# Ten of the 32 pieces of w_out decoded in MoE slots 2 to 5 and kept in DRAM, decode steps at fixed places, and the last selection ahead of its table

## The chip, the cores and the metric

The kernel runs on one core of a Trainium2 chip. The metric is the device time of one execution in microseconds, the median of several runs. A profiled execution has a time of its own, and its span runs from the first to the last instruction. The engines are TensorE (PE in the rows, PEld its weight loads), VectorE (DVE), ScalarE (ACT), GpSimd (POOL) and SyncE (SP), which issues most of the DMAs. Each engine works through its own instructions in order.

## The reference

Three layers in a row; the data are float32, but the last layer's weights come as float64.

```python
# 1: windowed attention, batch 4, 8 heads, 576 positions, 64 wide
attn = softmax(where(mask, q @ k.T / 8, -1e9))      # plain heads, then heads with dilation 4
x = (attn @ v).transpose(0, 2, 1, 3).reshape(2304, 512)
# 2: mixture of experts, one expert of 8 for each token
logits = x @ w_gate + modality_bias[modality_id]
e = argmax(logits); gate = softmax(logits)[e]
x = gate * (relu(x @ w1[e]) @ w2[e])                # w1: 512 x 1024, w2: 1024 x 512
# 3: the last layer
h = relu(x @ w_in)                                  # w_in: 512 x 2048
out = (h * h) @ w_out                               # w_out: 2048 x 512
```

## The kernel before, in words

All matrix products run on values split into a high and a low part (`hi`, `lo`), three matmuls for each product: hi x hi, hi x lo, lo x hi.

**Attention** is pipelined over 48 units of 96 queries (`schedule`, units counted by `i`, `nu` = 48). As the tokens of a batch are done, a side task routes them: `route` finds each token's expert and its place among that expert's tokens, and its end fills a table from slot and row to token (one-hot rows `rhot`, `val`, one matmul into `psi`, then `tbl`). `select` then finds which expert and which column of the table each MoE slot has (`esel`), and writes `itab`, from which `Moe.begin` on GpSimd reads a slot's token numbers (`sc`) and gathers its rows (`gx`). The side task yields a cost for every step, and `LATE[b]` zeros hold it back for as many units ahead of the table's matmul.

**The MoE** works on slots of 128 tokens of one expert, 18 or more in all (`Moe.main(j)`): layer one (`l1`, 24 matmuls, a yield after every third), transposing of the next slot's rows (`tx`, giving `xh` and `xl`), layer two of the slot before (`l2`, 24 matmuls), transposing of the hidden rows (`th`, giving `hth` and `htl`). Where a slot has another expert, its weights are loaded on SyncE (`stage`) and split on ScalarE and VectorE (`split`), both guarded by a branch. Slots 0 to 5 run between the last units of attention and after them (`moe.slots(0, NA)` as `fill`), slots 6 to 17 in a second loop in `body`; slots beyond these run under a branch (`extras`), and one does here.

**Decoding.** Float64 weights are turned into float32 pairs in pieces of 128 x 256 numbers. A step of the generator `decode` issues the DMA of one piece (`raw`) on SyncE and works on earlier pieces: an absolute value on ScalarE (`dm`), four passes on VectorE (`da`), the high part on ScalarE (`woh` or `wih`) and the low part, a subtraction, on GpSimd (`wol` or `wil`). The 32 pieces of w_in are decoded in slots 6 to 17, one step at each yield of cost 0 in the second loop. The 32 pieces of w_out, two to each 128-row block f of w_out, are decoded in block 0 of the last stage.

**The last stage** (`Ffn.run`) takes 6 blocks of 384 tokens. For each block and each of 16 values f: `l1` (12 matmuls of 384 columns, three banks in turn), `h1` (ReLU on ScalarE into `fr`, square into `fsq`), `h2` (`fhh` on ScalarE, `fhl` on VectorE), and with a lag of two to six values of f `l2` (9 matmuls of 512 columns, which need `woh` and `wol` of that f). In block 0 the order is written by hand, with two or three decode steps to each f. The squares of block 0 with f above 3 are on GpSimd, all others on VectorE. `Ffn.prep(1)` transposes block 1's rows near the end of block 0.

Of the kernel before, what the change touches and what calls it, by code (L numbers as in the profile page):

```python
# [26 lines left out]
FF = 2048  # L27
# [36 lines left out]
@with_exitstack  # L64
def body(ctx, tc, ins, out):
    nc = tc.nc
    const = ctx.enter_context(tc.tile_pool(name="const", bufs=1))
    dram = ctx.enter_context(tc.tile_pool(name="dram", bufs=1, space=bass.MemoryType.DRAM))
    psum = ctx.enter_context(tc.tile_pool(name="psum", bufs=1, space=PSUM))
    g = Ctx()  # L70
    g.tc, g.nc, g.ins, g.out = tc, nc, ins, out
    g.xd = dram.tile([NT, XW], F32, name="xd")
    g.ya = dram.tile([NA * 128, XW], F32, name="ya")
    g.yb = dram.tile([NT - NA * 128 + 128, XW], F32, name="yb")
    g.bk = [psum.tile([128, 512], F32, name=f"bk{i}") for i in range(8)]
    g.ident = const.tile([128, 128], F32, name="ident")
    g.iota = const.tile([128, NCOL], F32, name="iota")
    g.esel = const.tile([1, 4, NSLOT], I32, name="esel")
    g.nsl = const.tile([1, 1], I32, name="nsl")

    with ExitStack() as mctx:
        moe = Moe(g, mctx)
        with ExitStack() as actx:
            att = Attention(g, actx)
            att.warm(9)
            with tc.manual_schedule():
                schedule(att, moe)
# [12 lines left out]
        ffn.run()  # L100
# [11 lines left out]
def schedule(att, moe):  # L112
    nu = B * UPB
    moe.banks((2, 4), (4, 2), (2, 2), (7, 7))
    side, fc, sc, hold, nxt, due = None, 0.0, 0.0, 0, 0, 0
    i = 0
# [70 lines left out]
    run(side or ())  # L187
    if due:
        moe.ready = NSLOT
        moe.pump()  # L190


class Attention:
    def __init__(self, g, ctx):
# [235 lines left out]
    def route(self, b):  # L430
# [98 lines left out]
        if b:  # L529
            off = new([128, NCOL], "roff")  # L530
            nc.vector.tensor_scalar(out=off, in0=psi, scalar1=float(b * S), scalar2=float(b * S), op0=ALU.mult, op1=ALU.min)
            nc.vector.tensor_tensor(out=self.tbl, in0=self.tbl, in1=off, op=ALU.add)

    def select(self, j0, n):
# [97 lines left out]
        it = g.moe.itab[{0: 0, 2: 1, 6: 2}[j0]]  # L632
        yield 0.12
        nc.vector.tensor_scalar(out=it, in0=self.tbl, scalar1=-1.0, scalar2=0.0, op0=ALU.add, op1=ALU.max)
        for j in range(j0, j0 + n):
            g.moe.itab_of[j] = it


class Moe:
# [80 lines left out]
    def l1(self, j):  # L720
        nc = self.g.nc
        for hf in range(2):
# [3 lines left out]
            for c in range(4):  # L726
                for a, w in ((self.xh, self.wh[0]), (self.xh, self.wl[0]), (self.xl, self.wh[0])):
# [4 lines left out]
                    if k % 3 == 0:  # L732
                        yield 0.65
# [16 lines left out]
    def l2(self, j):  # L750
# [83 lines left out]
NB, TB = 6, 3  # L834
NF = FF // 128
DN = 256
LAG0, LAG = 6, 2


class Ffn:  # L840
    def __init__(self, g, ctx):
# [9 lines left out]
        jobs = [(wi[:, :, 2 * w * i:2 * w * i + 2 * w], self.wih[:, :, w * i:w * i + w], self.wil[:, :, w * i:w * i + w])  # L851
                for i in range(FF // w)]
        self.steps = itertools.chain(self.decode(jobs), self.prep0())

    def decode(self, jobs):
        nc, dp = self.g.nc, self.pool
        n = DN
        raws, vals = {}, {}
        for i in range(len(jobs) + 5):
            if i < len(jobs):  # L860
                src = jobs[i][0]
                raws[i] = dp.tile([128, n, 2], I32, tag="raw", name="raw", bufs=3)
                nc.sync.dma_start(out=raws[i].rearrange("p n two -> p (n two)").rearrange("p (c x) -> p c x", c=src.shape[1]), in_=src)
            new, old, done = i - 2, i - 3, i - 4
            if 0 <= new < len(jobs):
                m = dp.tile([128, n], F32, tag="m", name="dm", bufs=2)
                nc.scalar.activation(out=m, in_=raws[new][:, :, 1].bitcast(F32), func=AF.Abs)  # L867
                a = dp.tile([128, n], I32, tag="a", name="da", bufs=4)
                nc.vector.tensor_scalar(out=a, in0=raws[new][:, :, 1], scalar1=3, scalar2=0x3FFFFFF8,  # L869
                                        op0=ALU.logical_shift_left, op1=ALU.bitwise_and)  # L870
                vals[new] = (a, m)
            if old in vals:
                a = vals[old][0]
                nc.vector.scalar_tensor_tensor(out=a, in0=raws.pop(old)[:, :, 0], scalar=29, in1=a, op0=ALU.logical_shift_right, op1=ALU.bitwise_or)  # L874
            if new in vals:
                a = vals[new][0]
                nc.vector.scalar_tensor_tensor(out=a, in0=raws[new][:, :, 1], scalar=-0x40000000, in1=a, op0=ALU.bitwise_and, op1=ALU.bitwise_or)  # L877
            if old in vals:
                a, m = vals[old]
                nc.vector.scalar_tensor_tensor(out=a.bitcast(F32), in0=m, scalar=TINY, in1=a.bitcast(F32), op0=ALU.is_ge, op1=ALU.mult)  # L880
            if done in vals:
                _, hi, lo = jobs[done]
                v = vals.pop(done)[0].bitcast(F32).rearrange("p (c f) -> p c f", c=hi.shape[1])
                nc.scalar.activation(out=hi, in_=v, func=AF.Copy)  # L884
                nc.gpsimd.tensor_tensor(out=lo, in0=v, in1=hi.bitcast(F32), op=ALU.subtract)  # L885
            yield
# [62 lines left out]
    def h1(self, blk, f):  # L949
# [5 lines left out]
        (nc.gpsimd if blk == 0 and f > 3 else nc.vector).tensor_tensor(out=s, in0=r, in1=r, op=ALU.mult)  # L955
# [11 lines left out]
    def run(self):  # L967
# [3 lines left out]
        def pool(name, bufs):  # L971
# [6 lines left out]
        steps = self.decode([(wo[:, f:f + 1, 2 * h * DN:2 * (h + 1) * DN], woh[:, f:f + 1, h * DN:(h + 1) * DN], wol[:, f:f + 1, h * DN:(h + 1) * DN])  # L978
                             for f in range(NF) for h in range(DM // DN)])
# [104 lines left out]
```

## Time and profile before

| | us |
|---|---|
| median of 3 runs (813.43 to 816.45) | 816.21 |
| profiled execution, its time | 815.87 |
| profiled execution, its span | 814.1 |
| TensorE busy | 784.6 |
| VectorE busy | 418.9 |
| ScalarE busy | 325.1 |
| GpSimd busy | 173.9 |
| mean granted TensorE clock, share of full speed | 0.99 |

Busy times are sums over the whole span. The kernel goes through stages with different limits, so a stage is read from its own window. A matmul's end is modelled, so a stretch in which TensorE is shown busy may still contain short waits; the length of a stretch with known work tells more.

### The profile page before, as it was taken

What the parts mean: (1) busy time and instruction counts of PE and PEld (TensorE: products, weight loads), DVE (VectorE), ACT (ScalarE), POOL (GpSimd) and SP (SyncE); (2) the same over time, 40 slices, a digit from 0 to 9 for tenths busy, and PEclk for the clock granted to TensorE, in tenths of its full rate; (3) what the DMA queues carried; (4) which work ended last, traced back from release to release, by engine and by line L of the source; (5) the groups of instructions that cost most, each with busy time, mean ns of one, the idle gap of its engine ahead of it and who ended that gap; (6) DMA issues with size and microseconds to landing.
All of it is one profiled execution on the core that took longest, in us unless ns stands there. A gap on an engine that the chain in (4) does not pass through costs nothing.

```text
span 814.1 us, 12599 instructions
## 1 busy us (share of the span) xinstructions
PE 784.6 (96%) x4273; PEld 671.7 (83%) x4273; DVE 418.9 (51%) x1124; ACT 325.1 (40%) x779; POOL 173.9 (21%) x234
## 2 busy tenths in 40 slices
PE   8999987899999999998989899999999999999996
PEld 5888866788888888887877799989989989998995
DVE  5787888444257777441799942242242233224222
ACT  5777766232245554541444522232232222223221
POOL 4254731231123333110255610010000001001001
PEclk9999998999999999999999999999999999999999
DMA  7766681201234443722245410010001001001001
GB/s 225 188 177 163 177 279 43 68 27 46 72 118 119 140 130 100 247 91 72 80 115 147 127 39 26 1 52 27 1 13 39 27 14 39 1 0 39 1 1 39
DMA packets 44810, 67.40 MB, mean 83 GB/s; under 512 B 6816, under 2 KB 28672, under 8 KB 44224
## 3 DMA queue, kind: packets, MB, share of 16 engines
q1 hardware_dynamic: 38720, 50.75, 21.6%
q0 software_dynamic: 3280, 10.76, 4.3%
q10 hardware_dynamic: 2736, 4.99, 1.6%
q8 instruction: 35, 0.57, 0.3%
q14 instruction: 39, 0.32, 0.1%
HBM read 129.65 MB, written 14.44 MB: 177 GB/s over the span
## 4 chain that ended last, share of the span: by engine, by line
issue 40%; DVE 5%; PE 2%; DMA 2%; POOL 1%; ACT 1%; POOLq 0%; ACTq 0%; DVEq 0%; SPq 0%
DMA raw<-in_wo 2%; POOL out L995 1%; DVE da L880 1%; PE bk L945 1%; DVE fhl L964 1%; DVE da L874 1%; DVE da L869 1%; PE bk L758 1%; DVE da L877 1%; PE bk L990 1%; ACT dm L867 0%; ACT woh L884 0%; DVE fsq L955 0%; DVE yl L932 0%; DVE fout L994 0%
## 5 line engine op out<-in xcount | busy, mean ns | idle before, releaser
L955 DVE TENSOR_TENSOR fsq<-fr 128x384 f32<-128x384 f32 x84 | 46.9, 559 | 173.3 <-ACT fr L953 173.3
L945 PE MATMUL bk<-yh,wih 128*128 128x384 f32 x384 | 130.7, 340 | 3.2 <-ACTq L827 1.6
L945 PE MATMUL bk<-yl,wih 128*128 128x384 f32 x384 | 130.3, 339 | 1.3 <-DVE yl L932 1.3
L945 PE MATMUL bk<-yh,wil 128*128 128x384 f32 x384 | 129.9, 338 | 0.0
L953 ACT ACTIVATE fr<-bk 128x384 f32<-128x384 f32 x96 | 46.9, 488 | 187.9 <-PE bk L945 187.3
L990 PE MATMUL bk<-woh,fhh 128*128 128x512 f32 x288 | 114.6, 398 | 2.7 <-ACT woh L884 2.7
L990 PE MATMUL bk<-wol,fhh 128*128 128x512 f32 x288 | 113.4, 394 | 2.9 <-POOL wol L885 2.9
L990 PE MATMUL bk<-woh,fhl 128*128 128x512 f32 x288 | 113.3, 393 | 0.0
L995 POOL DMA_INDIRECT out<-fout,fidx x18 | 18.1, 1006 | 323.3 <-DVE fout L994 320.5
L945 PEld LDWEIGHTS bk<-yh,wih 128*128 128x128 f32 x384 | 72.6, 189 | 8.3 <-ACT yh L931 2.2
L964 DVE TENSOR_TENSOR fhl<-fsq,fhh 128x384 fp32r<-128x384 f32 x96 | 55.4, 578 | 45.0 <-ACT fhh L963 44.7
L945 PEld LDWEIGHTS bk<-yl,wih 128*128 128x128 f32 x384 | 72.7, 189 | 5.8 <-DVE yl L932 2.6
L945 PEld LDWEIGHTS bk<-yh,wil 128*128 128x128 f32 x384 | 72.7, 189 | 0.0
L963 ACT ACTIVATE fhh<-fsq 128x384 fp32r<-128x384 f32 x96 | 50.4, 525 | 50.2 <-DVE fsq L955 48.7
L990 PEld LDWEIGHTS bk<-wol,fhh 128*128 128x128 f32 x288 | 54.1, 188 | 14.2 <-POOL wol L885 5.9
L728 PE MATMUL bk<-w1h,xh 128*128 128x512 f32 x152 | 64.1, 421 | 0.8 <-DVE htl L744 0.8
L990 PEld LDWEIGHTS bk<-woh,fhl 128*128 128x128 f32 x288 | 54.0, 188 | 12.9 <-DVE fhl L964 0.4
L990 PEld LDWEIGHTS bk<-woh,fhh 128*128 128x128 f32 x288 | 54.1, 188 | 12.2 <-ACT woh L884 4.2
L728 PE MATMUL bk<-w1l,xh 128*128 128x512 f32 x152 | 61.6, 405 | 0.0
L728 PE MATMUL bk<-w1h,xl 128*128 128x512 f32 x152 | 61.5, 404 | 0.0
L758 PE MATMUL bk<-w2h,hth 128*128 128x512 f32 x152 | 61.0, 401 | 0.0
L758 PE MATMUL bk<-w2h,htl 128*128 128x512 f32 x152 | 59.5, 391 | 0.0
(173 smaller groups left out, 1375.9 us busy)
## 6 DMA issues: line engine op xcount, KB each, us to landing
st<-in_w SPq DMA_DIRECT2D x41, 2048.0 KB
raw<-in_wi SPq DMA_DIRECT2D x32, 256.0 KB
raw<-in_wo SPq DMA_DIRECT2D x32, 256.0 KB
v<-in_v SPq DMA_DIRECT2D x7, 780.0 KB
q<-in_q SPq DMA_DIRECT2D x7, 576.0 KB
kd<-in_k SPq DMA_DIRECT2D x14, 288.0 KB
xd<-x SPq DMA_DIRECT2D x40, 96.0 KB
yb<-y ACTq DMA_DIRECT2D x13, 256.5 KB
```

The source lines that it names most:

```text
L728: nc.tensor.matmul(ps, a[:, c, :], w[:, c, sl], start=k == 0, stop=k == 11)
L758: nc.tensor.matmul(ps, a[:, c, :], w[:, c, :], start=k == 0, stop=k == 23)
L869: nc.vector.tensor_scalar(out=a, in0=raws[new][:, :, 1], scalar1=3, scalar2=0x3FFFFFF8, op0=ALU.logical_shift_left, op1=ALU.bitwise_and)
L874: nc.vector.scalar_tensor_tensor(out=a, in0=raws.pop(old)[:, :, 0], scalar=29, in1=a, op0=ALU.logical_shift_right, op1=ALU.bitwise_or)
L877: nc.vector.scalar_tensor_tensor(out=a, in0=raws[new][:, :, 1], scalar=-0x40000000, in1=a, op0=ALU.bitwise_and, op1=ALU.bitwise_or)
L945: nc.tensor.matmul(ps, w[:, c, f * 128:(f + 1) * 128], a[:, c, :], start=k == 0, stop=k == 11)
L953: nc.scalar.activation(out=r, in_=ps, func=AF.Relu)
L955: (nc.gpsimd if blk == 0 and f > 3 else nc.vector).tensor_tensor(out=s, in0=r, in1=r, op=ALU.mult)
L963: nc.scalar.activation(out=hh, in_=s, func=AF.Copy)
L964: nc.vector.tensor_tensor(out=hl, in0=s, in1=hh.bitcast(F32), op=ALU.subtract)
L990: nc.tensor.matmul(acc[t], a[:, sl], w[:, f, :], start=f == 0 and j == 0, stop=f == NF - 1 and j == 2)
L995: dma = nc.gpsimd.indirect_dma_start(out=out, out_offset=bass.IndirectOffsetOnAxis(ap=self.idx[:, i:i + 1].bitcast(U32), axis=0), in_=o, i ...
```

## The change

The change has four parts. First, ten pieces of w_out (f = 0 to 4, `NE` = 5) are decoded by a new class `Early` while slots 2 to 5 run, stored to two DRAM tensors (`wod`), and loaded from there into `woh` and `wol` at the start of block 0 (`back`). Block 0 decodes the other 22, with one or two steps to each f. Second, a decode step is taken at marked yields (`MARK`): after the third matmul of each half of layer one and after the third and the fifteenth of layer two, four in a slot, for w_in too. Third, `route` is cut into `route`, `onehots` and `table`, and a new `batch` strings them together, so that only for the last batch `select` stands ahead of the table (`LATE` goes from 7 to 4 zeros there). Fourth, all squares are on VectorE. The pools of attention that only its units use are closed earlier, to make room for `Early`.

```diff
-LATE = (5, 5, 2, 7)
+LATE = (5, 5, 2, 4)
+    g.wod = [dram.tile([NE, 128, DM], F32, name=f"wo{i}") for i in range(2)]
...
             for cost in moe.slots(NA, NTT):
-                if not cost:
+                if cost == MARK:
                     ffn.side()
...
             else:
                 fc -= c
+                if early and c == MARK:
+                    early.step()
...
+        if i == nu + 6:
+            att.units.close()
+            early = Early(g)
...
-            side = itertools.chain(att.route(nxt), att.select(*WAVES[nxt - 1]) if nxt else ())
+            side = att.batch(nxt)
...
+    def batch(self, b):
+        moe = self.g.moe
+        yield from self.route(b)
+        if b < B - 1:
+            yield from self.table(b)
+        if b:
+            j0, n = WAVES[b - 1]
+            yield from self.select(j0, n)
+            for j in range(j0, j0 + n):
+                moe.itab_of[j] = moe.itab[b - 1]
+        if b == B - 1:
+            yield from self.table(b)
+        if b:
+            yield 0.12
+            self.g.nc.vector.tensor_scalar(out=moe.itab[b - 1], in0=self.tbl, scalar1=-1.0, scalar2=0.0, op0=ALU.add, op1=ALU.max)
...
                     if k % 3 == 0:
-                        yield 0.65
+                        yield MARK if k == 3 else 0.65
...
                 if k % 3 == 0 and k < 24:
-                    yield 0.65
+                    yield MARK if k in (3, 15) else 0.65
...
+class Early:
...
+        jobs = [(wo[:, f:f + 1, 2 * h * DN:2 * (h + 1) * DN], self.halves) for f in range(NE) for h in range(DM // DN)]
+        self.steps = decode(g.nc, self.pool, jobs, self.store)
...
+    def halves(self):
+        return [self.pool.tile([128, 1, DN], F32R, tag=t, name=t) for t in ("eh", "el")]
...
+    def store(self, i, hi, lo):
+        f, h = divmod(i, DM // DN)
+        for d, t in zip(self.g.wod, (hi, lo)):
+            self.g.nc.sync.dma_start(out=d[f, :, h * DN:(h + 1) * DN], in_=t[:, 0, :].bitcast(F32))
...
-        (nc.gpsimd if blk == 0 and f > 3 else nc.vector).tensor_tensor(out=s, in0=r, in1=r, op=ALU.mult)
+        nc.vector.tensor_tensor(out=s, in0=r, in1=r, op=ALU.mult)
...
+        def back(*fs):
+            for f in fs:
+                for t, d in zip((woh, wol), g.wod):
+                    nc.sync.dma_start(out=t[:, f, :].bitcast(F32), in_=d[f])
...
                     self.l1(0, i)
-                if i != 1:
+                if i < NE:
+                    back(i)
+                if i != 2:
                     next(steps, None)
                 if i:
                     self.h2(0, i - 1)
-                if i != 1:
-                    next(steps, None)
                 self.h1(0, i)
-                if i > 2 and i % 2:
+                if i > 2 and i % 4:
                     next(steps, None)
```

What stands in the engines' queues is shown at three places; numbers after a name tell tiles apart.

SyncE at the start of block 0: first the kernel before, where the loads of w_out for decoding begin at once.

```order
L863 DMA raw_6628<-in_wo 128x512 [waits DMAHW4_49,DVE_49,PE_49]
L863 DMA raw_6630<-in_wo 128x512 [waits DMAHW5_49]
L863 DMA raw_6656<-in_wo 128x512 [waits DMAHW6_49]
L863 DMA raw_6667<-in_wo 128x512 [waits DMAHW4_49,DMAHW7_49,DVE_49,Activation_49]
L863 DMA raw_6692<-in_wo 128x512 [waits DMAHW0_49,DMAHW5_49,DVE_49,Activation_49]
```

The same place in the changed kernel, with the ten loads from `wo0` and `wo1`.

```order
L1050 DMA woh_6784<-wo0_66 128x512 [waits DMAHW3_49,DMAHW4_49,DMAHW2_49,DMAHW5_49,DMAHW1_49,DMAHW6_49,DMAHW0_49,DMAHW7_49,DVE_49,Activation_49]
L1050 DMA wol_6785<-wo1_67 128x512 [waits DMAHW3_49,PE_49]
L881 DMA raw_6790<-in_wo 128x512
L1050 DMA woh_6784<-wo0_66 128x512
L1050 DMA wol_6785<-wo1_67 128x512 [waits DMAHW6_49]
L881 DMA raw_6798<-in_wo 128x512
L1050 DMA woh_6784<-wo0_66 128x512 [waits DMAHW0_49]
L1050 DMA wol_6785<-wo1_67 128x512 [waits DMAHW1_49]
L1050 DMA woh_6784<-wo0_66 128x512 [waits DMAHW2_49]
L1050 DMA wol_6785<-wo1_67 128x512 [waits DMAHW3_49]
L881 DMA raw_6844<-in_wo 128x512 [waits DMAHW4_49]
```

The first raw piece now stands behind a load that waits for TensorE, and the third is the eleventh in the queue.

VectorE in block 0, from `fhl` of f = 7 to `fhl` of f = 8, in the kernel before.

```order
L964 TENSOR_TENSOR fhl_6974<-fsq_6928,fhh_6973 128x384
L869 TENSOR_SCALAR da_6981<-raw_6930 128x256
L874 SCALAR_TENSOR_TENSOR da_6966<-raw_6915,da_6966 128x256
L877 SCALAR_TENSOR_TENSOR da_6981<-raw_6930,da_6981 128x256
L880 SCALAR_TENSOR_TENSOR da_6966<-dm_6964,da_6966 128x256
L869 TENSOR_SCALAR da_7034<-raw_6962 128x256
L874 SCALAR_TENSOR_TENSOR da_6981<-raw_6930,da_6981 128x256
L877 SCALAR_TENSOR_TENSOR da_7034<-raw_6962,da_7034 128x256
L880 SCALAR_TENSOR_TENSOR da_6981<-dm_6979,da_6981 128x256
L964 TENSOR_TENSOR fhl_7042<-fsq_6990,fhh_7041 128x384
```

The same place in the changed kernel.

```order
L1029 TENSOR_TENSOR fhl_7078<-fsq_7032,fhh_7077 128x384
L1020 TENSOR_TENSOR fsq_7083<-fr_7081 128x384
L887 TENSOR_SCALAR da_7127<-raw_7034 128x256
L892 SCALAR_TENSOR_TENSOR da_7070<-raw_7015,da_7070 128x256
L895 SCALAR_TENSOR_TENSOR da_7127<-raw_7034,da_7127 128x256
L898 SCALAR_TENSOR_TENSOR da_7070<-dm_7068,da_7070 128x256
L1029 TENSOR_TENSOR fhl_7135<-fsq_7083,fhh_7134 128x384
```

One decode step is gone from between them, and the square has come in. Elsewhere in the block there are two steps where three or two stood.

VectorE in slot 4, where the last batch's table is finished, in the kernel before.

```order
L528 TENSOR_TENSOR tbl_146<-bk5_71,tbl_146 128x144
L531 TENSOR_SCALAR roff_2938<-bk5_71 128x144
L532 TENSOR_TENSOR tbl_146<-tbl_146,roff_2938 128x144
L544 TENSOR_SCALAR sci_2941<-carry_141 1x8
L547 TENSOR_SCALAR scj_2943<-sci_2941 1x8
L550 TENSOR_TENSOR sav_2945<-scj_2943,taken_143 1x8
```

The same place in the changed kernel.

```order
L551 TENSOR_TENSOR tbl_151<-bk5_73,tbl_151 128x144
L554 TENSOR_SCALAR roff_3075<-bk5_73 128x144
L555 TENSOR_TENSOR tbl_151<-tbl_151,roff_3075 128x144
L571 TENSOR_SCALAR itab2_108<-tbl_151 128x144
L887 TENSOR_SCALAR da_3090<-raw_2986 128x256
L892 SCALAR_TENSOR_TENSOR da_3051<-raw_2959,da_3051 128x256
L895 SCALAR_TENSOR_TENSOR da_3090<-raw_2986,da_3090 128x256
L898 SCALAR_TENSOR_TENSOR da_3051<-dm_3049,da_3051 128x256
```

The selection, which began there (`sci` and on), has moved ahead to slots 2 and 3, `itab` follows on the table, and a decode step of w_out stands behind it. TensorE's matmuls keep their order but for the transposes of block 0's rows, which move by a few matmuls.

## Rows read from the trace of the kernel before

**Rows 1.** The page, part 1: busy time of each engine over the span.
```profile
PE 784.6 (96%) x4273; PEld 671.7 (83%) x4273; DVE 418.9 (51%) x1124; ACT 325.1 (40%) x779; POOL 173.9 (21%) x234
```

**Rows 2.** Windows: last-stage blocks 0 and 1 (window; each engine's busy us).
```profile
core 0: us, PE busy (x) PEld busy (x) DVE busy (x) ACT busy (x) POOL busy (x), PEclk, DMA share, GB/s
389.62:472.77 83.15, 74.07 (x350) 62.22 (x348) 74.43 (x162) 41.18 (x104) 39.01 (x44) 0.98 0.41 115
472.77:540.89 68.12, 68.12 (x350) 61.41 (x348) 21.90 (x42) 17.75 (x35) 3.10 (x3) 1.00 0.07 24
```

**Rows 3.** Waits in block 0: waiter, line, releaser: total us, times, longest.
```profile
PEld bk L990 <- POOL wol L885: 5.9, 9, 0.8
PEld bk L990 <- ACT woh L884: 4.2, 4, 1.3
...
PE bk L990 <- POOL wol L885: 2.9, 8, 0.5
PE bk L990 <- ACT woh L884: 2.7, 4, 1.0
```

**Rows 4.** Groups of VectorE in block 0 (count, busy us, mean ns, idle before).
```profile
L880 DVE SCALAR_TENSOR_TENSOR da<-dm,da 128x256 f32<-128x256 f32 x32 | 21.0, 656 | 0.0
L877 DVE SCALAR_TENSOR_TENSOR da<-raw,da 128x256 int32<-128x256 int32 x32 | 17.5, 548 | 0.0
L874 DVE SCALAR_TENSOR_TENSOR da<-raw,da 128x256 int32<-128x256 int32 x32 | 16.4, 512 | 0.0
L869 DVE TENSOR_SCALAR da<-raw 128x256 int32<-128x256 int32 x32 | 12.3, 383 | 2.5 <-DMA raw<-in_wo 2.5
L964 DVE TENSOR_TENSOR fhl<-fsq,fhh 128x384 fp32r<-128x384 f32 x18 | 11.9, 662 | 3.7 <-ACT fhh L963 3.4
L955 DVE TENSOR_TENSOR fsq<-fr 128x384 f32<-128x384 f32 x6 | 3.3, 552 | 10.0 <-ACT fr L953 10.0
```

**Rows 5.** Groups of GpSimd in block 0.
```profile
L885 POOL TENSOR_TENSOR wol<-da,woh 128x256 fp32r<-128x256 f32 x32 | 28.1, 879 | 55.1 <-ACT woh L884 42.2 <-DVE da L877 10.3 <-DVE da L869 2.6
L955 POOL TENSOR_TENSOR fsq<-fr 128x384 f32<-128x384 f32 x12 | 11.4, 947 | 0.0
```

**Rows 6.** Timeline of VectorE and GpSimd at 405 us (start us, us).
```profile
405.88 0.95 DVE L877 SCALAR_TENSOR_TENSOR da<-raw,da 128x256 int32<-128x256 int32 x1
...
407.72 0.28 DVE L869 TENSOR_SCALAR da<-raw 128x256 int32<-128x256 int32 x1
407.92 0.41 DVE L874 SCALAR_TENSOR_TENSOR da<-raw,da 128x256 int32<-128x256 int32 x1
...
405.81 0.75 POOL L885 TENSOR_TENSOR wol<-da,woh 128x256 fp32r<-128x256 f32 x1 [1.14 <-ACT woh L884]
```

**Rows 7.** Windows, columns as in rows 2: MoE slots 2, 3, 4, 5 and 10.
```profile
163.73:176.85 13.12, 13.12 (x72) 10.62 (x70) 6.63 (x32) 3.65 (x8) 1.73 (x3) 1.00 0.08 20
176.85:189.25 12.40, 12.40 (x63) 10.23 (x62) 2.41 (x7) 3.45 (x7) 6.81 (x10) 1.00 0.06 23
189.25:202.11 12.86, 12.86 (x70) 10.51 (x68) 7.87 (x40) 3.47 (x7) 0.63 (x2) 1.00 0.14 44
202.11:214.52 12.41, 12.41 (x63) 10.24 (x62) 2.33 (x7) 3.46 (x7) 4.09 (x7) 1.00 0.44 126
264.15:276.55 12.40, 12.40 (x63) 10.24 (x62) 9.74 (x26) 6.45 (x15) 4.54 (x7) 1.00 0.46 133
```

**Rows 8.** Windows, columns as in rows 2: a stop of TensorE and what followed.
```profile
457.85:460.62 2.77, 0.45 (x3) 0.19 (x2) 2.77 (x7) 1.67 (x6) 1.21 (x2) 1.00 0.50 144
460.66:464.08 3.42, 3.42 (x11) 3.42 (x12) 3.42 (x9) 1.56 (x5) 1.79 (x2) 0.50 0.38 98
```

**Rows 9.** Heavy loads (last column GB/s); GpSimd's wait; SyncE's issues of w_out.
```profile
342.00:348.00 6.00, 6.00 (x32) 4.98 (x32) 1.83 (x6) 2.47 (x5) 0.56 (x2) 1.00 0.92 345
...
POOL sc L706 <- DVE itab L634: 17.0, 1, 17.0
...
L863 SPq DMA_DIRECT2D raw<-in_wo x32: 327/328/541, 382.0 to 458.8; - x32
```

More of the change, by code (lines that the diff above doesn't have):

```diff
@@ L187, in schedule @@
     run(side or ())
+    early.close()
     if due:
@@ L206, in __init__ @@
         self.idb = cmask[:, 3 * KT:]
-        self.tri = ac.tile([QT, QT], F16, name="tri")
-        self.ones = ac.tile([QT, QT], F16, name="ones")
-        self.wg = ac.tile([128, 4, 2 * E], F32R, name="wg")
+        self.tri = al.tile([QT, QT], F16, name="tri")
+        self.ones = al.tile([QT, QT], F16, name="ones")
+        self.wg = al.tile([128, 4, 2 * E], F32R, name="wg")
         wraw = ac.tile([128, 4, E], F32, name="wraw")
@@ L514, in route, with onehots @@
         nc.vector.tensor_copy(rf, ri)
-        rhot, val = new([QT, TPB, 128], "rhot", F16), new([QT, TPB, NCOL], "rval", F16)
+        self.hots = cf, rf, new([QT, TPB, 128], "rhot", F16), new([QT, TPB, NCOL], "rval", F16)
+        if b != 2:
+            yield from self.onehots(b)
+    def onehots(self, b):
+        nc, iota = self.g.nc, self.g.iota
+        cf, rf, rhot, val = self.hots
         eng = nc.vector if b == 2 else nc.gpsimd
         for i in range(TPB):
-            if b == 2:
-                yield 0.5
+            yield 0.5 if b == 2 else 0.01
             eng.tensor_scalar(out=rhot[:, i, :], in0=iota[:QT, :128], scalar1=rf[:, i:i + 1], scalar2=None, op0=ALU.is_equal)
@@ L522, in route, with table @@
                               scalar2=self.tok[:, i:i + 1], op0=ALU.is_equal, op1=ALU.mult)
+    def table(self, b):
+        nc, rt = self.g.nc, self.rt
+        rhot, val = self.hots[2:]
+        if b == 2:
+            yield from self.onehots(b)
         for _ in range(LATE[b]):
@@ L529, in route @@
         if b:
-            off = new([128, NCOL], "roff")
+            off = rt.tile([128, NCOL], F32, tag="roff", name="roff")
             nc.vector.tensor_scalar(out=off, in0=psi, scalar1=float(b * S), scalar2=float(b * S), op0=ALU.mult, op1=ALU.min)
             nc.vector.tensor_tensor(out=self.tbl, in0=self.tbl, in1=off, op=ALU.add)
+    def batch(self, b):
[13 more added lines that the diff above has]
+            self.g.nc.vector.tensor_scalar(out=moe.itab[b - 1], in0=self.tbl, scalar1=-1.0, scalar2=0.0, op0=ALU.add, op1=ALU.max)
     def select(self, j0, n):
@@ L630, in select @@
             nc.vector.tensor_tensor(out=self.taken, in0=self.taken, in1=tk, op=ALU.add)
[L632 to L636, printed above, removed]
 class Moe:
@@ L834 @@
 NB, TB = 6, 3
+NE = 5
 NF = FF // 128
@@ L837, with decode @@
 LAG0, LAG = 6, 2
+def decode(nc, dp, jobs, store=None):
+    n = DN
+    raws, vals, outs = {}, {}, {}
+    for i in range(len(jobs) + 6):
+        if i < len(jobs):
+            src = jobs[i][0]
+            raws[i] = dp.tile([128, n, 2], I32, tag="raw", name="raw", bufs=3)
+            nc.sync.dma_start(out=raws[i].rearrange("p n two -> p (n two)").rearrange("p (c x) -> p c x", c=src.shape[1]), in_=src)
+        new, old, done = i - 2, i - 3, i - 4
+        if 0 <= new < len(jobs):
+            m = dp.tile([128, n], F32, tag="m", name="dm", bufs=2)
+            nc.scalar.activation(out=m, in_=raws[new][:, :, 1].bitcast(F32), func=AF.Abs)
+            a = dp.tile([128, n], I32, tag="a", name="da", bufs=4)
+            nc.vector.tensor_scalar(out=a, in0=raws[new][:, :, 1], scalar1=3, scalar2=0x3FFFFFF8,
+                                    op0=ALU.logical_shift_left, op1=ALU.bitwise_and)
+            vals[new] = (a, m)
+        if old in vals:
+            a = vals[old][0]
+            nc.vector.scalar_tensor_tensor(out=a, in0=raws.pop(old)[:, :, 0], scalar=29, in1=a, op0=ALU.logical_shift_right, op1=ALU.bitwise_or)
+        if new in vals:
+            a = vals[new][0]
+            nc.vector.scalar_tensor_tensor(out=a, in0=raws[new][:, :, 1], scalar=-0x40000000, in1=a, op0=ALU.bitwise_and, op1=ALU.bitwise_or)
+        if old in vals:
+            a, m = vals[old]
+            nc.vector.scalar_tensor_tensor(out=a.bitcast(F32), in0=m, scalar=TINY, in1=a.bitcast(F32), op0=ALU.is_ge, op1=ALU.mult)
+        if done in vals:
+            hi, lo = outs[done] = jobs[done][1]()
+            v = vals.pop(done)[0].bitcast(F32).rearrange("p (c f) -> p c f", c=hi.shape[1])
+            nc.scalar.activation(out=hi, in_=v, func=AF.Copy)
+            nc.gpsimd.tensor_tensor(out=lo, in0=v, in1=hi.bitcast(F32), op=ALU.subtract)
+        if store and done - 1 in outs:
+            store(done - 1, *outs.pop(done - 1))
+        yield
@@ new lines, with __init__, step, close @@
+class Early:
+    def __init__(self, g):
+        self.g = g
+        self.cm = g.tc.tile_pool(name="fe", bufs=2, side="right")
+        self.pool = self.cm.__enter__()
+        wo = g.ins["wo"].bitcast(I32)
+        jobs = [(wo[:, f:f + 1, 2 * h * DN:2 * (h + 1) * DN], self.halves) for f in range(NE) for h in range(DM // DN)]
[6 more added lines that the diff above has]
+            self.g.nc.sync.dma_start(out=d[f, :, h * DN:(h + 1) * DN], in_=t[:, 0, :].bitcast(F32))
+    def step(self):
+        next(self.steps, None)
+    def close(self):
+        for _ in self.steps:
+            pass
+        self.cm.__exit__(None, None, None)
@@ L850, in __init__ @@
         wi = g.ins["wi"].bitcast(I32)
[L851 to L886, printed above, removed]
@@ L888, in side, with cols @@
+        def cols(i):
+            return lambda: (self.wih[:, :, w * i:w * i + w], self.wil[:, :, w * i:w * i + w])
+        jobs = [(wi[:, :, 2 * w * i:2 * w * i + 2 * w], cols(i)) for i in range(FF // w)]
+        self.steps = itertools.chain(decode(g.nc, self.pool, jobs), self.prep0())
     def side(self):
@@ L977, in run, with part @@
         wo = g.ins["wo"].bitcast(I32)
-        steps = self.decode([(wo[:, f:f + 1, 2 * h * DN:2 * (h + 1) * DN], woh[:, f:f + 1, h * DN:(h + 1) * DN], wol[:, f:f + 1, h * DN:(h + 1) * DN])
-                             for f in range(NF) for h in range(DM // DN)])
+        def part(f, h):
+            return lambda: (woh[:, f:f + 1, h * DN:(h + 1) * DN], wol[:, f:f + 1, h * DN:(h + 1) * DN])
+        def back(*fs):
+            for f in fs:
+                for t, d in zip((woh, wol), g.wod):
+                    nc.sync.dma_start(out=t[:, f, :].bitcast(F32), in_=d[f])
+        steps = decode(nc, self.pool, [(wo[:, f:f + 1, 2 * h * DN:2 * (h + 1) * DN], part(f, h))
+                                       for f in range(NE, NF) for h in range(DM // DN)])
         self.hp = hp
```

28 lines of the change are left out of this document (16 added, 12 removed).

## The prediction, made before the changed kernel ran

> **What bounds the kernel now.** I read the page first, then windows cut by stage, then the waits of the stage that stood out. The page says that TensorE is busy 96% of the span [rows 1], so a change is worth something only where TensorE waits or runs slowly. That is found by cutting the span into equal pieces of work. The last stage runs six blocks of the same TensorE work: 16 first-layer groups, 16 second-layer groups, 12 transposes. Cut from one block's third first-layer group to the next block's, block 1 takes 68.12 us with TensorE busy throughout; block 0 takes 83.15 us with TensorE busy 74.07 and VectorE busy 74.43 [rows 2]. So block 0 holds **15.03 us** that the same work does not need. The MoE slots hold none: slots 3 and 5, without decoding, take 12.40 and 12.41 us with TensorE busy throughout, and slot 10, with four decode steps, 12.40 [rows 7]; slots 2 and 4 are longer by the remaining attention and routing matmuls, and TensorE is busy there too.
>
> What ends the waits of block 0 is the decoding of w_out: TensorE and its weight loads wait for `wol` (GpSimd) and `woh` (ScalarE), 5.9, 4.2, 2.9 and 2.7 us [rows 3]. Both come off a chain whose slow member is VectorE: a piece takes four passes there, 21.0 + 17.5 + 16.4 + 12.3 = 67.2 us for 32 pieces, 2.10 us a piece [rows 4]. Alone, a pass takes 0.28 or 0.41 us, 1.51 us a piece; one that starts beside a subtraction on GpSimd takes 0.95 us [rows 6]. Over 44 GpSimd operations in block 0 [rows 5] the stretch is (67.2 - 32 x 1.51) / 44 = 0.43 us each. TensorE's clock is part of the 15.03 us too: after a window in which it was busy 0.45 of 2.77 us, the granted clock stands at 0.50, the lower of its two levels (1.2 of 2.4 GHz), for 3.42 us [rows 8], which costs half of that, 1.7 us.
>
> **The change part by part.**
>
> *Ten pieces leave block 0.* The four passes of 22 pieces with one GpSimd operation each: 22 x 1.51 + 22 x 0.43 = 42.7 us, where 67.2 stood. The twelve squares of f above 3 move from GpSimd (0.947 us each, rows 5) to VectorE at 0.552: 18 x 0.552 = 9.9 us, where 3.3 stood [rows 4]. `fhl` stays at 11.9. The groups of rows 4 go from 82.4 to 64.5 us; their ends overlap (74.43 busy against 82.4 summed, 0.90), so VectorE's busy time falls to about 58 us. Before, block 0 lasted 83.15 - 74.43 = 8.7 us longer than VectorE was busy (its start, and waits inside the chain). With the same 8.7 us, VectorE would let block 0 end after 67 us, and TensorE needs 68.1: TensorE becomes the bound, barely. The bounds of this term are 15.03 us of gain (no wait left) and 7 us (each GpSimd operation holding a VectorE pass for its whole 0.88 us, worked out under the rivals). I take 15.03 less 1.0 for what stays, because the work is uneven. At f = 3 to 7 VectorE has nine steps and ten operations on hidden tiles, about (9 x 1.94 + 5 x 1.21) x 0.90 = 21 us, where TensorE has eight groups of 68.1 / 32 = 2.1 us, 17 us. It falls some 4 us behind there. The cover is that these pieces are due four values of f (4.3 us each) after they are decoded, the last ones still one, and that three banks let the first layer run two groups ahead. Without that cover the 4 us would be paid.
>
> *Reading back.* The ten loads of 256 KB come first in SyncE's queue. `wol` overwrites the MoE's `w2h`, so it waits for the last MoE matmul, at 389.6, and the first load of w_out for decoding, issued at 382.0 before [rows 9], now stands behind it. Ten loads and the first four raw pieces are 3.7 MB; at the 345 GB/s of a window of heavy loads [rows 9] they are in by 400.5. The pair for f = 0 is first in the queue and is wanted only after four first-layer groups (8 us), so it is hidden; the third raw piece, eleventh in the queue, comes at about 399.5 and is wanted by VectorE, by the prices above, at about 399. Price: 0 to 1 us, inside the 1.0 above; 5 us if VectorE's whole chain starts that much later.
>
> *Ten pieces enter slots 2 to 5.* A step costs VectorE (9.74 - 2.33) / 4 = 1.85 us, from slot 10 against slot 5 [rows 7]. Slot 4 has 5.5 us more than slot 5, nearly all of it selection, which leaves it; with four steps it comes to about 10.7 of 12.86. Slot 2 gains most of that selection and half a step: about 12 of 13.12. Slot 3, with four steps and the selection's end, comes to about 10.8, slot 5 to 8. The work that hides this is TensorE's own, 12.4 us a slot; what VectorE owes it (`xl`, `htl`) is wanted one layer, 5 us, later. Price: nothing; if VectorE ran over in all four slots, 1 to 2 us in each. ScalarE has 3.5 of 12.4 us busy and GpSimd at most 6.81 [rows 7]; the twenty stores and the loads go beside DMA shares of 0.06 to 0.44. What queues behind SyncE's stores are the guarded weight loads, the raw pieces and the reads of the slot table; in GpSimd's queue the subtractions of later pieces stand behind the gather of slot 6, which waits for `itab`.
>
> *Selection ahead of its table* makes the last `itab` ready earlier in slot 4. Slot 5 already ran at 12.41 us with TensorE full, so this gives nothing, and takes nothing as long as the table's matmul keeps its place, which it does. *Decode steps of w_in at fixed places*: slots with four steps already take 12.40 us. Nothing either way; the twelve transposes of block 0's inputs move by a few matmuls and are the same twelve.
>
> **The sum**, against the profiled execution's own time: 815.87 - 15.03 + 1.0 = 801.8 us. That execution lies 0.3 us below the median of the runs, so I forecast **802 us**.
>
> **The rivals.**
>
> *VectorE stays level with TensorE in block 0* (about 808.5). For it: 58 + 8.7 is close to 68.1, and the squares come to the engine that was short. If each GpSimd operation held a pass for its whole 0.88 us [rows 5], the passes would sum to 33.2 + 19.3, and the groups to 74.3 us; times 0.90 plus 8.7 is 75.6, so 7.5 us stay: 815.87 - 7.5 = 808.4. Against it: the measured stretch is half of that, 0.43, and it came with 44 operations, not 22. The Trainium skill has the rule behind it (SBUF — State Buffer, "Who interferes with whom"): a VectorE instruction with two SBUF inputs and a GpSimd instruction that reads SBUF exclude each other, and the loser blocks for the whole instruction. The pairs in rows 6 agree that passes are held; the mean of 0.43 us says that mostly the tail of an operation is waited out. By the rule at its full length, this rival's time.
>
> *The reading back delays the decoding* (about 806). Raw pieces arrive 5 us later than I think, VectorE starts as much later, and about 4 us stay beside my 1.0. For it: one queue in order, behind a wait for TensorE. Against: DMA share in block 0 is 0.41 [rows 2], and the raw pieces cost VectorE 2.5 us of waiting in all [rows 4].
>
> *Slots 2 to 5 lengthen* (about 808). Four slots by 1.5 us. For it: slot 2 comes near its length. Against: slot 10 with 9.74 us of VectorE lost nothing.
>
> *Slower than before* (about 820). GpSimd waited 17.0 us for `itab` [rows 9]. Now subtractions stand in that queue; with one held, its store on SyncE is held, behind it the raw pieces, then VectorE's next pass and, behind that in VectorE's order, `htl`. TensorE has about 5 us of cover; it decides when the hold passes that. A hold of 17 us would then cost 12, and the stop would bring a stretch at the lower clock as in rows 8, 2 us more; with half as much again at the gathers that follow, 19 us against the 15 gained. Against: `itab` now follows directly on its table, and the first five subtractions stand ahead of that gather.
>
> **How the numbers follow.** My case 0.76; VectorE level 0.09; reading back 0.08; slots 0.04; slower 0.03. The low end is the whole 15.03 us and the spread of the runs below the median, 799. The high end takes in the first three rivals, 809; less than 1 in 10 lies outside. Within 0.5% is 4.1 us, about what a measurement can tell from no change. All cases but the last lie below 812.1: faster 0.94, same 0.03, slower 0.03.
>
> **What the new profile would show.** Block 0, cut in the same way, at 68 to 70 us with clock 1.00 and no stretch at the lower level; the four passes at about 43 us for 22 pieces and VectorE busy about 58; waits for `wol` and `woh` under 2 us in sum; the slots still at 12.4 us, with 8 to 12 us of VectorE in slots 2 to 5. I am wrong if block 0 still shows second-layer groups that wait for `wol`, if the passes stay near 2.1 us a piece, or if a slot from 2 to 5 is longer than before.

## The result, and the profile after

The changed kernel took 806.64 us (median of 5 runs, 803.13 to 808.73), the kernel before beside it 815.76 (5 runs, 813.19 to 816.45): a ratio of 0.9896, 95% interval 0.9861 to 0.993. Measured again, beside further runs of the kernel before, it gave 806.98 against 816.5, 0.9896 (0.9876 to 0.9916). So it is faster by 1%, some 9 us, where I had forecast 14. The profiled execution is the fastest of the changed kernel's eleven runs, 803.13 us with a span of 801.4 (their median is 806.93); a second profile, below, is of a run of 808.43 us.

Block 0 did what was forecast. Windows of the changed kernel, blocks 0 and 1, cut as in [rows 2]:

```profile
core 0: us, PE busy (x) PEld busy (x) DVE busy (x) ACT busy (x) POOL busy (x), PEclk, DMA share, GB/s
391.84:460.03 68.19, 68.19 (x349) 61.37 (x348) 56.25 (x134) 33.89 (x84) 24.74 (x22) 1.00 0.49 147
460.03:528.15 68.12, 68.12 (x349) 61.41 (x348) 21.88 (x42) 17.74 (x35) 3.08 (x3) 1.00 0.07 24
```

83.15 us have become 68.19, TensorE is busy in all of them at the full clock (2.4 GHz), and block 0 is now as long as block 1. In the waits of this window TensorE no longer appears behind `wol` or `woh`, as it did in [rows 3]; all that is listed for it is 0.6 us of its weight loads, for `fr`. What VectorE does there, by groups, for [rows 4]:

```profile
...
L895 DVE SCALAR_TENSOR_TENSOR da<-raw,da 128x256 int32<-128x256 int32 x22 | 11.3, 514 | 0.0
L892 DVE SCALAR_TENSOR_TENSOR da<-raw,da 128x256 int32<-128x256 int32 x22 | 11.3, 513 | 0.0
L1020 DVE TENSOR_TENSOR fsq<-fr 128x384 f32<-128x384 f32 x18 | 9.9, 549 | 8.5 <-ACT fr L1018 8.5
L898 DVE SCALAR_TENSOR_TENSOR da<-dm,da 128x256 f32<-128x256 f32 x22 | 9.7, 439 | 0.0
L887 DVE TENSOR_SCALAR da<-raw 128x256 int32<-128x256 int32 x22 | 8.3, 377 | 5.9 <-DMA raw<-in_wo 5.3 <-POOL wol L903 0.6
```

The four passes sum to 40.6 us (forecast 42.7), the squares to 9.9 (forecast 9.9). Before the first pass VectorE waits 5.3 us for raw pieces where [rows 4] has 2.5; the ten loads that are read back now stand ahead of these pieces. TensorE did not wait for either.

The loss is in the slots. Slots 2 to 6 of the changed kernel, for [rows 7]:

```profile
162.09:175.17 13.08, 13.08 (x72) 10.61 (x70) 8.25 (x41) 4.09 (x9) 1.06 (x2) 1.00 0.44 121
175.17:187.58 12.41, 12.41 (x64) 10.24 (x61) 11.02 (x45) 4.91 (x12) 10.70 (x13) 1.00 0.21 65
187.58:201.10 13.52, 13.21 (x69) 10.48 (x68) 6.22 (x20) 5.47 (x12) 2.85 (x5) 1.00 0.59 175
201.10:216.68 15.58, 13.24 (x62) 10.29 (x61) 8.72 (x24) 5.90 (x14) 6.53 (x10) 1.00 0.50 154
216.68:229.09 12.41, 12.41 (x64) 10.24 (x62) 4.26 (x13) 5.08 (x10) 3.20 (x5) 1.00 0.50 143
```

Slot 3 carries 11.02 us of VectorE and loses nothing; slots 4 and 5 carry less and are 0.66 and 3.17 us longer than before. So it is not VectorE's load. What stands in their waits (window 187.58 to 216.68: waiter, line, releaser; total, times, longest):

```profile
POOL el L903 <- ACT eh L902: 18.7, 6, 4.4
ACT eh L902 <- DMA wo<-eh: 10.4, 4, 3.3
DVE htl L777 <- ACT hth L776: 6.4, 2, 3.6
DVE xl L749 <- ACTq L727: 5.5, 2, 3.2
...
PEld bk L791 <- ACTq L727: 1.8, 1, 1.8
PE bk L791 <- ACTq L727: 1.6, 1, 1.6
```

Read from the second row: ScalarE, about to write `eh`, waits 10.4 us in all until an earlier piece's store has read that buffer. The pool has two buffers, and `decode` issues a piece's store one step after the piece is written, so only one decode step lies between a store and the write that wants its buffer back. ScalarE takes its instructions in order, so `hth`, `xh` and `hr` of the slot stand behind that write, and TensorE's second layer (L791) waits for them. (TensorE's release is put down to L727, the guard of `split` that follows in ScalarE's queue; in slot 5 `hth` ends at 209.51 us and TensorE goes on at 209.60.)

The first profile also gains 1.7 us in slots 0 and 1, which is chance: the clock, shown under the fifth experiment.

### The profile page after: what moved, and what is told of

Same layout as the page of the kernel before. It is cut to its first block, busy times and chain, and to the rows that moved or that the text cites. A ratio compares the mean times of both kernels' runs of the same rounds, so it can differ in the third digit from the quotient of the medians.

```text
span 801.4 us, 12644 instructions
## 1 busy us (share of the span) xinstructions
PE 777.8 (97%) x4273; PEld 668.9 (83%) x4273; DVE 411.8 (51%) x1136; ACT 325.0 (41%) x779; POOL 170.1 (21%) x222
## 4 chain that ended last, share of the span: by engine, by line
issue 40%; PE 9%; POOL 1%; DVE 0%; POOLq 0%; ACT 0%; ACTq 0%
PE bk L1010 4%; PE bk L1064 4%; POOL out L1069 1%; PE bk L791 1%; DVE fout L1068 0%; PE bk L993 0%; POOLq L1154 0%; DVE fsq L1020 0%; DVE fhl L1029 0%; ACT fr L1018 0%; POOLq L1069 0%; ACTq L1018 0%
## 5 line engine op out<-in xcount | busy, mean ns | idle before, releaser
L1020 DVE TENSOR_TENSOR fsq<-fr 128x384 f32<-128x384 f32 x96 | 53.5, 557 | 170.6 <-ACT fr L1018 170.4
L791 PE MATMUL bk<-w2h,hth 128*128 128x512 f32 x152 | 61.1, 402 | 1.6 <-ACTq L727 1.6
L791 PE MATMUL bk<-w2l,hth 128*128 128x512 f32 x152 | 59.3, 390 | 0.4 <-DVEq L727 0.4
```

The costliest lines, as they stand in the source:

```text
L1020: nc.vector.tensor_tensor(out=s, in0=r, in1=r, op=ALU.mult)
```

## The experiments

My theory after the result: block 0 was bound by the decoding and is now bound by TensorE; what is missing was lost in slots 4 and 5, where ScalarE stands behind a store. Rivals: VectorE or SyncE's queue is overloaded there; or GpSimd, whose gathers stand behind subtractions, holds TensorE.

**The changed kernel again.** 

> The changed kernel once more, for a second profile beside the runs below. If the loss in slots 4 and 5 (13.52 and 15.58 us where 12.86 and 12.41 stood) belongs to the program's order, it stands there again within 0.5 us, with ScalarE waiting for the stores of `eh`; if it was chance of one execution, the two slots differ by over 1 us from the first profile. Block 0 at 68.2 us either way. Time 804 to 809.

Measured 806.98 us (6 runs, 805.9 to 810.58). Block 0 takes 67.96 us, slot 4 13.05 and slot 5 19.48. Slots 4 and 5 of this profile, and below them slot 5's stop and what followed (windows):

```profile
188.62:201.67 13.05, 13.05 (x69) 10.48 (x67) 6.15 (x20) 5.38 (x12) 2.48 (x5) 1.00 0.62 181
201.67:221.15 19.48, 15.74 (x63) 12.01 (x61) 8.18 (x24) 6.88 (x15) 8.63 (x12) 0.82 0.46 142
...
208.40:211.90 3.50, 0.25 (x4) 0.03 (x1) 0.58 (x1) 2.08 (x4) 0.72 (x1) 0.83 0.52 197
211.90:217.30 5.40, 5.27 (x12) 3.80 (x13) 2.95 (x10) 2.04 (x6) 1.05 (x2) 0.50 0.32 102
```

TensorE is busy 0.25 us in 3.50, and then runs at half clock. So the loss stands here too, with ScalarE waiting for the store of `eh`, and its size varies: 3.8 us in the first profile's two slots, 7.3 here (32.53 against 25.27). The expectation's "within 0.5 us" held for slot 4 and failed for slot 5, by the clock and a longer stop; taken by its letter, a difference over 1 us spoke for chance, and what decides against that is the experiments below. The stop in the timelines of ScalarE, SyncE (issues) and GpSimd (start us, us, what, idle time before):

```profile
204.59 0.43 ACT L885 ACTIVATE dm<-raw 128x256 f32<-128x256 f32 x1 [1.39 <-issue]
209.28 0.42 ACT L902 ACTIVATE eh<-da 128x256 fp32r<-128x256 f32 x1 [4.26 <-DMA wo<-eh]
209.61 0.67 ACT L796 ACTIVATE y<-bk,lrow 128x512 f32<-128x512 f32 x1
...
210.69 1.09 ACT L776 ACTIVATE hth<-bk 128x512 fp32r<-128x512 f32 x2 [0.41 <-ACT y L796]
...
199.09 0.38 SPq L924 DMA_DIRECT2D wo<-el  x1
203.71 0.00 SPq L708 DMA_DIRECT2D st<-in_w  x1
204.44 0.01 SPq L881 DMA_DIRECT2D raw<-in_wo  x1
204.45 0.23 SPq L924 DMA_DIRECT2D wo<-eh  x1
...
201.59 1.06 POOL L740 DMA_INDIRECT gx<-xd,sc  x1 [0.80 <-DMA wo<-eh]
...
203.12 0.98 POOL L740 DMA_INDIRECT gx<-xd,sc  x1 [0.27 <-POOL sc L739]
...
204.82 1.07 POOL L740 DMA_INDIRECT gx<-xd,sc  x1 [0.27 <-POOL sc L739]
205.91 0.98 POOL L903 TENSOR_TENSOR el<-da,eh 128x256 fp32r<-128x256 f32 x1
```

When the last wave's selection is ready, three slots begin at once. SyncE issues no transfer from 199.5 to 203.7 us (the trace has it reading slot numbers there), so the store of `eh` leaves at 204.45, right behind a 2 MB weight load and a raw piece, and ScalarE is let go at 209.28. GpSimd issues three gathers from 201.59 to 205.89, and its subtraction waits behind them. `hth` starts at 210.69, more than 2 us after TensorE stopped, and ends at 211.78; TensorE goes on at 211.87.

**Four buffers for `eh` and `el`.**

```diff
-        return [self.pool.tile([128, 1, DN], F32R, tag=t, name=t) for t in ("eh", "el")]
+        return [self.pool.tile([128, 1, DN], F32R, tag=t, name=t, bufs=4) for t in ("eh", "el")]
```

> Four buffers for `eh` and `el` in place of two, nothing else. Theory (ScalarE stands in order behind a store that has not ended, and with it `hr`, `xh` and `hth`): the waits of the line of `eh` for the store fall from 10.4 us to under 3, slot 5 comes back to 12.4 to 12.8 us and slot 4 to 12.9, the time falls by 3 to 4 us against the changed kernel. Rival (VectorE has too much in slots 4 and 5): both slots stay at 13.5 and 15.6, no change. Rival (SyncE's queue as a whole is late, weights too): slots shorten by less than half.

Measured 799.37 us (798.98 to 801.08), ratio to before 0.9795 (0.9779 to 0.9811): 7.6 us under the changed kernel on the same chip. Slots 4 and 5 in windows:

```profile
188.15:201.02 12.87, 12.87 (x70) 10.50 (x68) 10.14 (x29) 7.26 (x17) 6.78 (x10) 1.00 0.74 222
201.02:213.42 12.40, 12.40 (x63) 10.24 (x62) 5.90 (x15) 4.82 (x11) 5.11 (x7) 1.00 0.66 205
```

Both slots are as short as before the change, and no wait of `eh` for a store is listed in them. Slot 4 has more VectorE work (10.14 us) than in the changed kernel. The rival of VectorE's load has fallen. The gain is double the expected 3 to 4 us, as the expectation was read from the mildest execution (3.8 us).

**The stores in GpSimd's queue, two buffers.**

```diff
-            self.g.nc.sync.dma_start(out=d[f, :, h * DN:(h + 1) * DN], in_=t[:, 0, :].bitcast(F32))
+            self.g.nc.gpsimd.dma_start(out=d[f, :, h * DN:(h + 1) * DN], in_=t[:, 0, :].bitcast(F32))
```

> The twenty stores of the early pieces go out of GpSimd's queue, where they follow the subtraction that they store, in place of SyncE's; two buffers as in the changed kernel. Theory that the stores are late because they stand behind guarded weight loads on SyncE: slots 4 and 5 fall to under 13.2 us each, 2 to 4 us less in all. If the store's own duration from issue to landing is the cause, with no queue ahead of it: the slots stay over 14 in the sum's excess. If GpSimd's own wait for `itab` holds them: slot 5 or 6 gets longer, 3 to 10 us.

Measured 809.24 us (0.9919, 0.9902 to 0.9935); slot 4 takes 12.85 us and slot 5 20.45. GpSimd's and ScalarE's timelines:

```profile
202.80 1.20 POOL L740 DMA_INDIRECT gx<-xd,sc  x1 [0.68 <-POOL sc L739]
...
206.07 0.97 POOL L740 DMA_INDIRECT gx<-xd,sc  x1 [0.27 <-POOL sc L739]
207.06 0.74 POOL L903 TENSOR_TENSOR el<-da,eh 128x256 fp32r<-128x256 f32 x1
207.73 0.60 POOL L924 DMA_DIRECT2D wo<-eh  x1
...
210.24 0.42 ACT L902 ACTIVATE eh<-da 128x256 fp32r<-128x256 f32 x1 [6.65 <-DMA wo<-eh]
```

My first expectation failed: SyncE's queue is not the only late one. Here the same three gathers stand ahead of the store, and ScalarE waits 6.65 us. Moving the store changes which queue is late; the buffers decide whether ScalarE notices.

**The squares of f above 3 back on GpSimd in block 0.**

```diff
-        nc.vector.tensor_tensor(out=s, in0=r, in1=r, op=ALU.mult)
+        (nc.gpsimd if blk == 0 and f > 3 else nc.vector).tensor_tensor(out=s, in0=r, in1=r, op=ALU.mult)
```

> The squares of f above 3 in block 0 go back to GpSimd (12 of 0.95 us), all else as changed. If VectorE is the nearly full engine of block 0 (58 us by my sum, and 67 with the start): without 12 x 0.552 us of squares it is freer, but 12 more GpSimd operations stretch its passes by about 12 x 0.43, so block 0 stays at 68 to 69 us, TensorE the bound: no change. Rival (the squares on GpSimd delay `fsq` and `fhl`, or stretch the passes by their whole 0.9 us): block 0 at 70 to 75 us, 2 to 7 us slower than the changed kernel.

Block 0 in a window:

```profile
396.35:466.75 70.40, 68.89 (x350) 61.29 (x348) 57.92 (x122) 33.82 (x84) 33.01 (x34) 1.00 0.46 143
```

70.40 us, 2.2 longer than with the squares on VectorE: my own expectation (68 to 69) failed, and the rival's (70 to 75) held at its low end. VectorE is busy longer (57.92 against 56.25 us) although twelve squares left it: the four passes sum to 46.7 us in place of 40.6. TensorE's longest wait in the block is for VectorE's `fhl`, as the rival has it:

```profile
PE bk L1064 <- DVE fhl L1029: 1.2, 1, 1.2
```

The time is 808.77 us, 1.8 above the changed kernel beside it, with intervals that overlap; the window is the evidence.

**Only the order of selection and the fixed places.** `NE = 0`, and block 0's decode steps and squares as in the kernel before.

```diff
-NE = 5
+NE = 0
...
-                if i != 2:
+                if i != 1:
                     next(steps, None)
                 if i:
                     self.h2(0, i - 1)
+                if i != 1:
+                    next(steps, None)
                 self.h1(0, i)
-                if i > 2 and i % 4:
+                if i > 2 and i % 2:
```

> No piece of w_out decoded early: block 0 has its 32 pieces, its three decode steps and its squares on GpSimd as before the change; what stays of the change is the selection in front of the last table and the fixed places of the decode steps. Theory (these two are worth nothing, all gain is block 0): block 0 at 83 us, slots 4 and 5 at 12.9 and 12.4, time within 1 us of the kernel before. Rival (they are worth some 1.6 us, since slots 0 and 1 took 18.4 and 17.2 us before and 17.8 and 16.2 after): those two slots at the shorter lengths, time 1 to 2 us under the kernel before.

> The kernel before, for a second profile. If slots 0 and 1 are longer in it by its order, they stand at 18.4 and 17.2 us again; if the stretch at the lower clock at 146.6 to 150.1 us was chance, slot 1 comes at about 16.2. Block 0 at 82 to 84 us.

Measured 814.84 us (12 runs) against 815.58, ratio 0.9991 (0.9976 to 1.0007): no change. Block 0 takes 82.57 us, slots 4 and 5 12.87 and 12.41. The kernel before, profiled again at 814.11 us, took 83.11 us in block 0 and 17.32 and 16.16 us in slots 0 and 1. These two slots in the first profile of before, and then in the second:

```profile
128.10:146.49 18.39, 16.08 (x100) 12.69 (x99) 14.96 (x43) 11.66 (x29) 0.00 (x0) 0.87 0.06 18
146.49:163.73 17.24, 16.70 (x82) 13.18 (x83) 6.20 (x34) 3.27 (x7) 4.66 (x8) 0.90 0.27 74
```

```profile
128.38:145.70 17.32, 15.00 (x100) 12.12 (x99) 14.94 (x44) 11.65 (x29) 0.00 (x0) 0.93 0.07 20
145.70:161.86 16.16, 15.57 (x82) 11.88 (x83) 6.18 (x34) 3.27 (x7) 4.65 (x8) 1.00 0.30 79
```

The same program, the granted clock 0.90 in slot 1 once and 1.00 the other time: these 1 to 2 us come and go within one kernel and are not the change's.

**Three buffers; and six early pieces in place of ten, with four buffers.** The first sets `bufs=3` where the second experiment sets 4; the second:

```diff
-NE = 5
+NE = 3
...
-                if i > 2 and i % 4:
+                if i > 2:
```

> Three buffers for `eh` and `el`. Theory: a buffer is asked for again one piece later, about 3 us in slots with four steps; ScalarE's longest wait of 4.3 to 6.6 us at a store falls to 1 to 3 us, less than the one layer of cover that TensorE has (5 us), so at most 1 us stays in slots 4 and 5: within 1.5 us of the version with four. Rival (the delay of the stores is the burst's whole 5 to 6 us and three do not bridge it): slot 5 at 14 to 17 us.

> Four buffers, but six pieces early in place of ten, so that block 0 decodes 26 (with a decode step at each f above 2 in its second place). By my sum with the measured stretch: 26 x (1.51 + 0.34) + 9.9 + 11.8 = 69.8 us, times 0.90 is 63 busy, with 8.7 us of start 71.6: block 0 at 71 to 72 us, 3 to 4 us slower than the version with ten early. Rival (ten was more than needed, TensorE is the bound at 26 too): block 0 at 68.2 to 69, no change.

Three buffers: 801.48 us (0.9817, 0.979 to 0.9844), slots 4 and 5 at 12.87 and 12.40; one more buffer is enough. Six early pieces: 804.97 us (0.9871, 0.9847 to 0.9895). Block 0 of that kernel, and a row of the waits in it:

```profile
388.32:461.68 73.36, 69.94 (x349) 61.05 (x348) 63.26 (x149) 36.20 (x92) 25.37 (x26) 1.00 0.46 137
```

```profile
PEld bk L1064 <- POOL wol L903: 4.9, 6, 2.2
```

VectorE is busy 63.26 us, as summed (63), but the block lasts 73.36, not 71 to 72: the wait for `wol` is back. Ten pieces were not too many.

**Four buffers for one tile only.** `eh` four and `el` two; then `eh` two and `el` four; then four of both again. The first:

```diff
-        return [self.pool.tile([128, 1, DN], F32R, tag=t, name=t) for t in ("eh", "el")]
+        return [self.pool.tile([128, 1, DN], F32R, tag=t, name=t, bufs=n) for t, n in (("eh", 4), ("el", 2))]
```

> Four buffers for `eh` alone, two for `el`. Theory (the wait costs because ScalarE stands in it, with `hr`, `xh` and `hth` behind): as with four of both, slots 4 and 5 at 12.9 and 12.4, time 799 to 801.5. Rival (GpSimd's wait for the buffer of `el`, with the gathers of the next slots behind it, holds TensorE as well): slots 4 and 5 stay 2 us or more too long, 803 or more.

> Two buffers for `eh`, four for `el`: the same theory wants the changed kernel's loss back, slot 5 at 15 to 20 us and the time at 805 to 809; the rival wants it mostly gone, under 803.

> The version with four buffers of both once more, beside the two above: slots 4 and 5 at 12.9 and 12.4, time 799 to 801.5; a stretch at the lower clock in slots 0 and 1, where one appears, makes 1 to 2 us of that.

Measured on one chip: 800.55 us (0.9815, 0.9796 to 0.9834), 804.94 (0.9868, 0.9846 to 0.9889) and 801.72 (0.9824, 0.9806 to 0.9843). The wait at the store in the first, and in the second:

```profile
POOL el L903 <- DMA wo<-el: 6.4, 3, 4.4
```

```profile
POOL el L903 <- ACT eh L902: 20.3, 6, 4.5
ACT eh L902 <- DMA wo<-eh: 11.6, 4, 3.6
...
PEld bk L791 <- ACTq L727: 2.8, 1, 2.8
```

In the first GpSimd waits 6.4 us for its buffer and slots 4 and 5 are clean (12.86, 12.41). In the second ScalarE waits as in the changed kernel, and slots 4 and 5 take 13.52 and 19.27 us. So the wait costs because it stands in ScalarE's order; the rival of the gathers behind GpSimd has fallen. The second version's 804.94 lies just under its expected range (runs at 803.1 to 808.3), and the third's 801.72 just above its own, 799 to 801.5.

## Why the prediction was right in sign and 5 us off in size

The forecast was 802 us and 806.64 was measured. That this lies inside the stated range of 799 to 809 is luck: the upper end came from three rivals, and none of them happened with the cause that it names.

*Ten pieces leave block 0: right.* The term was 15.03 us of gain less 1.0. Measured 14.96 us in the first profile and 15.15 from second profile to second profile (83.11 to 67.96): the 1.0 was 0.1 or nothing. VectorE's 58 us were 56.25; the stretch for each GpSimd operation was (40.6 - 22 x 1.51) / 22 = 0.34 us in place of 0.43. The forecast "barely" was near the truth too: four pieces more and the block is 5.2 us longer (the run with six early pieces), twelve squares back on GpSimd and it is 2.2 longer.

*VectorE level in block 0 (808.5): refuted in its size.* By the Trainium skill (SBUF — State Buffer, "Who interferes with whom") whoever takes the shared ports first holds them for its whole instruction. A pass held for a whole operation by each of the 22 would make the passes 33.2 + 22 x 1.13 = 58 us, with GpSimd's mean of 1.13 us from the changed kernel's block 0 (24.74 us in 22); they took 40.6. GpSimd loses as well: its subtraction takes 0.74 us at 207.06 us of the run with stores in GpSimd's queue, where VectorE is idle. That both lose agrees with the rule; that a pass loses 0.34 us to an operation of 1.13 says that on average it waits out only part of one.

*Reading back: right.* VectorE waited 5.3 us for raw pieces before its first pass where 2.5 stood, and TensorE did not notice. (At the 345 GB/s of the forecast the eleventh transfer is in at about 398, not 399.5; nothing hangs on it.) *Selection ahead of its table, fixed places: right*, nothing (0.9991).

*Ten pieces enter slots 2 to 5, "Price: nothing": this step failed.* It summed VectorE's time, which was near in slot 3 (11.02 us of a forecast 10.8) and in slot 4 where nothing holds it (10.14 of 10.7), too high in slot 2 (8.25 of 12), and not what bound the slots. It named as cover that `xl` and `htl` are wanted one layer later. It gave ScalarE and the stores a busy share and a DMA share; it listed what queues behind the stores, but not what the stores queue behind, nor who waits for them. ScalarE's copy into `eh` needs a buffer that only a store releases, the store stands in SyncE's queue behind the start of three slots, and there were two buffers. That costs 3.8 us in the first profile and 7.3 to 8.0 in the four later ones with two buffers for `eh`; four buffers give back 7.6 beside the changed kernel, and by the ratio of their repeat (0.9824 for 0.9896) some 6. The prediction's own sign of being wrong, a slot from 2 to 5 longer than before, was seen. The rival "slots 2 to 5 lengthen" named the place and nearly the time (808), but with VectorE as its cause, and had 0.04. The rival "slower" had the queue behind the gathers, but led it by the raw pieces and VectorE instead of by the buffer and ScalarE, and put it at 820.

Without this wait the sum holds: 802 over 815.87 is 0.983, and the versions with `eh` free to run ahead gave 0.9795, 0.9815, 0.9817 and 0.9824.

What stays open is why one execution of the changed kernel stops only briefly in slot 5 (15.58 us) and the others longer; four later profiles with two buffers for `eh` all show 19.15 to 20.45 us. In the first profile the store of `eh` let ScalarE go 3.3 us after its issue (203.68 to 207.01), in the second 4.8.

A smaller loss stays unexplained too. Slot 16 takes 13.48 and 14.19 us in the two profiles of the changed kernel, against 13.28 before and 13.29 with no piece decoded early, and TensorE's weight loads wait there for block 0's rows (`fy<-ya`), 0.4 and 1.1 us. The prediction's sum has no term for these 0.2 to 0.9 us; no run separates the cause.

## What to carry to other kernels

A sum of busy times prices a moved step only if none of its instructions waits. For each tile that the step writes, ask who releases its buffer, in which queue that stands, what burst that queue serves, and what else stands behind the writer on its own engine; a third buffer for such tiles cost no time here, and took the ratio from 0.9896 to 0.9817. When a transfer is late, moving it to another queue may only find the same burst there. And one profile can be the mildest of many: look at a second before sizing a loss.

## What the runs showed of the chip beyond that

A store of 128 KB let ScalarE go 4.8 us after its issue (204.45 to 209.28) when a weight load of 2 MB and a raw piece had been issued within the 0.74 us ahead of it, and 2.5 us after (207.73 to 210.24) from GpSimd's queue, where those two had been issued 5 to 7 us before (201.17 and 202.43). So the shorter time need not be the queue's doing. The store's row on SyncE is 0.23 us long in the first. The Trainium skill (Perfetto Trace Analysis, "Per-instruction lifecycle: what the profiler-reported window actually captures") says that for a DMA the data's movement lies outside the reported window; the rows agree, 0.23 us against 4.8 until the buffer is free.

TensorE's clock: after a stop with 0.25 us busy in 3.50 the granted clock was 0.50 (1.2 GHz) in the next 5.4 us. In the first profile's slot 5 the stop left TensorE busy 1.82 of 3.80 us, and the clock stayed at 1.00:

```profile
207.70:211.50 3.80, 1.82 (x9) 1.14 (x7) 1.68 (x5) 2.62 (x6) 1.28 (x2) 1.00 0.33 123
```

So a stop with 1.6 times the idle time (3.25 us against 1.98) cost 2.2 times as much: slot 5 lost 3.17 us in the one and 7.07 in the other.
